# One bank for the attention sums, three common banks, and a rewritten opening order

## The chip, the cores and the metric

The kernel runs on one core of one Trainium2 chip. The metric is the device time of one execution in microseconds: the median of 16 runs is 722.01 (719.96 to 723.24). A profiled execution, recorded by the hardware, gives the times of single instructions. Engine names below are those of the profile: PE is TensorE (PEld its weight loads), DVE is VectorE, ACT is ScalarE, POOL is GpSimd, SP is SyncE. An L with a number is a line of the kernel.

## The reference

Causal attention with two kinds of heads, then a mixture of experts whose routing weights come from eight rounds of row and column normalization (Sinkhorn). Sizes: 4 batches, 8 heads, 768 positions, head width 64; 3072 tokens of width 512, 8 experts with an inner width of 1024.

```python
scores = scale * np.matmul(q, k.transpose(0, 1, 3, 2))
mask = np.where(retr, causal, causal & (is_sink | in_win))   # retrieval heads see all, others sinks and a window
a = np.exp(scores masked); a = a / a.sum(-1)
x = np.matmul(a, v)                                          # heads side by side: 3072 x 512
P = np.exp(x @ w_gate); 8 times: P /= P.sum(1); P /= P.sum(0); P *= N / E
out = sum over e of P[:, e] * (np.maximum(x @ w1[e], 0) @ w2[e])
```

## The kernel before

**Units and rounds.** Attention is cut into 24 units (b, g, u): batch b, a group g of 256 query positions, and half u of the heads (four heads, in two pairs a). A pair's scores over the keys it may see come in chunks of two key blocks: one chunk for g = 0, two for g = 1, three for g = 2. A task is one chunk of one pair, and a round is two tasks; there are 48 rounds, twelve per batch. A g = 0 unit takes one round, so two pairs end in it; in the later groups at most one pair ends in a round.

**What is done for a unit.** `emit_prep` (L249) transposes its keys and queries on PE (the tile `tr`) and copies them to `kT` on DVE (L263). `emit_scores` (L423) makes the score products (L450) into a tile `sc` of two banks, and returns two steps: the exponential on ACT (L459, PSUM to the SBUF tile `PT`), and the masking of `PT` on DVE (L468, L471). `gen_pv` (L282) makes the products of the exponentials with the values and a column of ones (L289, tile `pv`), and `normalize` inside it takes the reciprocal of the sums (L302) and multiplies (L303, into `xn`), both on DVE. `turn` (L310) transposes `xn` (L318, tile `xt`) and copies it on ACT to `xT` (L321), the experts' input.

**Fillers.** With half u = 1 of a group turned, `first_steps` (L348) queues the work of expert 0 on these 256 tokens: four first-layer steps (L357, eight products, counted as 1 each) and two second-layer steps (L371, eight products of 512 columns, counted as 2 each): 8 units per group, 96 in all. `fill(n)` takes steps from this queue, `spend(n)` (L502) tells how many units are to be left after round n. A first-layer step ends with a relu: on ACT (L362) where `late[0]` is true, else on DVE (L364). A second-layer step ends with a copy on ACT (L375). `emit_logits` (L333, tile `lgp`) makes the routing logits of a finished batch.

**PSUM.** Eight banks: `sc` two buffers of two banks, `pv` two buffers of one, and two banks under the tag "mo", which `tr`, `xt`, `lgp`, the fillers' `l1` and `l2` and the keep-warm products share in turn. `place_v` (L117), which brings the first batch's values to their place through PE, takes an `sc` buffer. Where a tile's buffers are all in use, the next writer waits for the reader of the oldest.

**Order.** The opening, from the first keep-warm products to the end of the sixth round's work, stands in a `manual_schedule` region for PE, DVE and ACT: each engine issues in the order in which the code is written. `keep_warm` (L275) adds products of 512 columns whose result nobody reads; the opening has 9 at the start and 19 later. From round 6 on (the loop `for n in range(6, rounds)`, outside the region) the framework's scheduler picks the order on each engine. POOL has its own written order of loads at the start; later loads are issued from `emit_scores`. `finish_sums` (L486) makes the value products of all pairs that are due, in the opening sometimes with the normalizing held back (`hold`). `make_far` (L236) and `make_far_all` (L222) spell out per-head factors that multiply the values of far key blocks (`emit_vfar`, L268).

**After attention** comes the Sinkhorn stretch: eight iterations on DVE, each with `fill(3)` and one small product; then the experts 1 to 7 in a seven-product scheme (L715 and L784), with PE as the engine that is never free.

Of the kernel before, what the change touches and what calls it, by code (L numbers as in the profile page):

```python
# [10 lines left out]
F32 = mybir.dt.float32  # L11
F16 = mybir.dt.float16
# [24 lines left out]
def kernel(  # L37
# [78 lines left out]

    def place_v(g):  # L117

        t = psA.tile([128, 2, 512], F32, tag="sc", bufs=2, name=f"vp_{g}")
        for n in range(2):  # L120
            rows = slice(64 * n, 64 * n + 64)
            for c in range(2):
                nc.tensor.matmul(
                    out=t[64 * c:64 * c + 64, n, :].rearrange("p (h d) -> p h d", h=H),
                    lhsT=ident16[rows, rows], rhs=vraw[g][rows, :, c, :], start=True, stop=True,
                )
        nc.scalar.activation(
            out=v_tile(0)[:, :, 2 * g:2 * g + 2, 0:D].rearrange("p h n d -> p n h d"),
            in_=t.rearrange("p n (h d) -> p n h d", h=H), func=AF.Copy, bias=0.0, scale=1.0,
        )  # L130

    def load_v_heads(b, h0, h1):
        for o in range(2):
# [85 lines left out]
                                    scalar2=None, op0=ALU.mult)  # L219
        nc.vector.tensor_copy(out=keep[:, 512:640], in_=keep[:, 256:384])  # L220

    def make_far_all():  # L222
        for n in range(2):
            nc.scalar.activation(
                out=farx[:, :, n], in_=farf[:, :, n].unsqueeze(2).broadcast_to([128, H, DV]),
                func=AF.Copy, bias=0.0, scale=1.0)
        nc.scalar.activation(out=farx[:, :, 2], in_=farx[:, :, 1], func=AF.Copy, bias=0.0, scale=1.0)

    def make_masks(js):
        for h in [2 * j + hh for j in js for hh in range(2)]:  # L230
# [5 lines left out]
    def make_far():  # L236

        for i in range(2):
            nc.scalar.activation(out=farf[:, :, i], in_=retf, func=AF.Copy, bias=0.0, scale=1.0)
        for rows in sinks:  # L240
            nc.vector.memset(farf[rows, :, 0], 1.0)

    wg16 = constp.tile([128, 4, E], F16, tag="wg16")

# [3 lines left out]

    def emit_prep(b, g, u):  # L249

        tr = psA.tile([128, 512], F32, tag="mo", bufs=2, name=f"tr_{b}_{g}_{u}").bitcast(F16)
        for i, src in enumerate(kq[b, g]):
            for a in range(2):
                for c in range(2):
                    for hh in range(2):
                        nc.tensor.transpose(
                            out=tr[64 * hh:64 * hh + 64, ts(4 * i + 2 * a + c, 128)],
                            in_=src[:, 4 * u + 2 * a + hh, c, :], identity=ident16,
                        )
        t = ap.tile([128, 2, 2, 256], F16, tag=f"kT{u}{g}", bufs=1 + (g == 0),  # L260
                    name=f"kT_{b}_{g}_{u}")
        kTs[b, g, u], qTs[b, g, u] = t[:, 0], t[:, 1]
        nc.vector.tensor_copy(  # L263
            out=t.rearrange("r i a (n c p) -> r (i a) c n p", c=2, p=64),
            in_=tr.rearrange("r (i c n p) -> r i c n p", i=4, c=2, p=64),
        )
# [7 lines left out]

    def keep_warm(lhsT, src, n):  # L275
        for _ in range(n):
            t = psA.tile([128, 512], F32, tag="mo", bufs=2, name="warm")
            nc.tensor.matmul(out=t[:, 0:src.shape[1]], lhsT=lhsT, rhs=src, start=True, stop=True)

    xns, turns = {}, []  # L280

    def gen_pv(b, g, u, a, PT, scale):  # L282

        pv = psA.tile([128, 2, 2, DV], F32, tag="pv", bufs=2, name=f"pv_{b}_{g}_{u}_{a}")
        vt, vf = vts[b], vfs.get(b)
        todo = pv_of(g)
        for i, (kj, far, sb, off) in enumerate(todo):
            for hh in range(2):
                nc.tensor.matmul(  # L289
                    out=pv[:, sb, hh, 0:D + 1], lhsT=PT[:, hh, off:off + 128],  # L290
                    rhs=(vf if far else vt)[:, 4 * u + 2 * a + hh, kj, 0:D + 1],
                    start=(i == 0 and hh == 0), stop=(i == len(todo) - 1 and hh == 1),
                    skip_group_check=True,
                )
            yield
        if a == 0:
            xns[b, g, u] = ap.tile([128, 2, 2, 2, D], F16, tag="xn", name=f"xn_{b}_{g}_{u}")
        xn = xns[b, g, u]

        def normalize():  # L300
            rc = ap.tile([128, 2, 2], F32, tag="rc", bufs=4, name=f"rc_{b}_{g}_{u}_{a}")
            nc.vector.reciprocal(out=rc, in_=pv[:, :, :, D])  # L302
            nc.vector.tensor_tensor(  # L303
                out=xn[:, a], in0=pv[:, :, :, 0:D],
                in1=rc.unsqueeze(3).broadcast_to([128, 2, 2, D]), op=ALU.mult)
            if a == 1:
                turns.append((b, g, u))
        scale.append(normalize)

    def turn():  # L310

        while turns:
            b, g, u = turns.pop(0)
            xn = xns.pop((b, g, u))
            xt = psA.tile([128, 512], F32, tag="mo", bufs=2, name=f"xt_{b}_{g}_{u}").bitcast(F16)
            for a in range(2):
                for sb in range(2):
                    nc.tensor.transpose(out=xt[:, ts(2 * a + sb, 128)], in_=xn[:, a, sb],  # L318
                                        identity=ident16)
            c0 = b * S + 256 * g  # L320
            nc.scalar.activation(  # L321
                out=xT[u][:, :, c0:c0 + 256], in_=xt[:, 0:512].rearrange("p (a c) -> p a c", a=2),
                func=AF.Copy, bias=0.0, scale=1.0)
            if u == 1:
                one, two = first_steps(b, g)
                at = 4 if (b, g) == (0, 1) else len(fillers)
                fillers[at:at] = one
                fillers.extend(two)

# [1 line left out]
    late = [False]  # L331

    def emit_logits(b):  # L333
        lgp = psA.tile([128, 512], F32, tag="mo", bufs=2, name=f"lgp_{b}")
# [12 lines left out]

    def first_steps(b, g):  # L348
# [2 lines left out]
        hT = [hp.tile([128, 512], F16, tag="hT", name=f"hT_0_{b}_{g}_{i}") for i in range(4)]  # L351

        def layer1(i):
            l1 = psA.tile([128, 512], F32, tag="mo", bufs=2, name="l1")
# [10 lines left out]
            return 1  # L365

        def layer2(sb):
            l2 = psA.tile([128, DM], F32, tag="mo", bufs=2, name="l2")
            for fc in range(8):
                o = 256 * (fc % 2) + 128 * sb  # L370
                nc.tensor.matmul(  # L371
# [111 lines left out]
            n -= done  # L483
            left[0] -= done

    def finish_sums(hold=False):  # L486
        held = []
        for (i, a), (gen, scale) in list(sums_of.items()):
            while run(gen, 1):
                pass  # L490
            del sums_of[i, a]
            held += scale
        if not hold:
            for f in held:
                f()
        return held


    rounds = len(tasks) // 2
    weights = [0] * 6 + [1] * (rounds - 6)  # L500

    def spend(n):  # L502
        fill(left[0] - (96 - 72 * sum(weights[:n + 1]) // sum(weights)))

    def sum_later(n):
        for i, a, ci in tasks[2 * n:2 * n + 2]:
# [19 lines left out]
    with tc.manual_schedule(engines=engines):  # L526
# [5 lines left out]
        round_first(4)  # L532
        r0 = scores(0)
        soften(r0, (0,))
        warm(3)
        make_masks((0, 1))
        emit_prep(*preps.pop())
        warm(2)
        place_v(0)
        r1 = scores(1)  # L540
        soften(r0, (1,))
        soften(r1, (0,))
        sum_later(0)
        warm(6)
        make_masks((2, 3))
        soften(r1, (1,))
        scale = finish_sums(True)
        emit_prep(*preps.pop())
        for f in scale:
            f()  # L550
        warm(4)
        sum_later(1)
        r2 = scores(2)
        soften(r2, (0,))
        turn()
        make_far_all()
        scale = finish_sums(True)
        soften(r2, (1,))
        for f in scale:
            f()  # L560
        sum_later(2)
        emit_prep(*preps.pop())
        emit_vfar(0, 1)
        warm(2)
        soften(scores(3))
        place_v(1)
        turn()
        finish_sums()
        sum_later(3)
        warm(2)  # L570
        soften(scores(4))
        turn()
        finish_sums()
        sum_later(4)
        soften(scores(5))
        turn()
        finish_sums()
        sum_later(5)
        emit_prep(*preps.pop())
    for n in range(6, rounds):  # L580
        soften(scores(n))
        if n == 7:
            place_v(2)
        if preps:
            emit_prep(*preps.pop())
        late[0] = n % 12 < 6
        turn()
        finish_sums()
        sum_later(n)
        if n % 12 == 2 and n > 12:  # L590
            emit_logits(n // 12 - 1)
# [308 lines left out]
```

The softmax here doesn't subtract the row's maximum and nothing guards it: scores larger than these inputs give would overflow.

## Time and profile before

| | |
|---|---|
| median of 16 runs | 722.01 us |
| the profiled execution | 719.76 us |
| its span, first to last instruction | 718.0 us |
| mean granted TensorE clock in the span | 0.993 |

Busy time in five stretches of the span, in us:

| stretch | PE | PEld | DVE | ACT | POOL |
|---|---|---|---|---|---|
| 31.0 to 58.3 (rounds of batch 0) | 25.14 | 16.57 | 18.59 | 16.96 | 7.89 |
| 58.3 to 97.4 (batch 1) | 37.02 | 24.72 | 21.77 | 29.14 | 9.09 |
| 97.4 to 136.0 (batch 2) | 36.58 | 24.80 | 21.38 | 28.81 | 4.47 |
| 136.0 to 168.0 (batch 3) | 31.18 | 20.72 | 16.89 | 24.80 | 0.00 |
| 168.0 to 192.0 (Sinkhorn) | 22.86 | 15.72 | 16.33 | 11.25 | 0.79 |

The batch borders are put roughly; the scheduler lets neighbouring rounds overlap. A row of the order of instructions reads: start, duration, engine, line, operation, what it writes and reads, shape, how many were merged; in brackets, how long the engine had been idle before it and what ended that idle time. Products are pipelined, so the busy time of PE includes their latency, and a PE that looks full may have short gaps. Idle time of an engine that isn't the one that everything waits for costs nothing.

### The profile page before, as it was taken

The numbers are of one execution on the slowest core, as the hardware profiler recorded it, in microseconds if no ns is written. First come the engines' busy times: TensorE is split into PE (matmuls) and PEld (weight loads), VectorE is DVE, ScalarE is ACT, GpSimd is POOL, SyncE is SP. The second block draws the span as 40 slices with busy tenths as digits, with TensorE's granted clock in tenths as the row PEclk, the third lists the DMA queues.
The fourth block names the chain that finished last, engine by engine and source line by source line (L and its number), as shares of the span: only waits on it lengthen the run. The fifth ranks groups of instructions, "written<-read, shape, count | busy, mean of one in ns | idle before, by whom it ended". The sixth has DMA issues, their size and how long they took to land.

```text
span 718.0 us, 17079 instructions
## 1 busy us (share of the span) xinstructions
PE 692.3 (96%) x6944; PEld 571.5 (80%) x6944; DVE 563.3 (78%) x1147; ACT 422.2 (59%) x787; POOL 151.2 (21%) x183
## 2 busy tenths in 40 slices
PE   7799999999999999999999999999999999999995
PEld 3466666666578888888888888888888888888884
DVE  6665465755779997888788878988898788877886
ACT  4767777685596555555555555555555555555550
POOL 7412040000011222212221212122221312121210
PEclk9999999999999999999999999999999999999999
DMA  9999393000443359434943495339543964245774
GB/s 179 178 175 104 31 105 31 2 1 2 76 69 63 59 85 162 78 54 72 164 87 55 74 148 96 68 60 150 101 74 56 145 107 78 48 80 111 147 158 123
DMA packets 84223, 65.61 MB, mean 91 GB/s; under 512 B 48304, under 2 KB 64688, under 8 KB 84144
## 3 DMA queue, kind: packets, MB, share of 16 engines
q0 software_dynamic: 74976, 57.17, 56.6%
q1 hardware_dynamic: 7536, 6.30, 3.7%
q8 instruction: 54, 0.88, 0.5%
q10 hardware_dynamic: 1632, 1.05, 0.5%
q14 instruction: 25, 0.20, 0.1%
HBM read 52.45 MB, written 6.29 MB: 82 GB/s over the span
## 4 chain that ended last, share of the span: by engine, by line
PE 67%; DVE 2%; issue 0%; ACT 0%; DVEq 0%
PE l1y L715 19%; PE l2y L784 19%; PE l2w L784 10%; PE l1w L715 10%; PE l2z L784 5%; PE l1z L715 5%; DVE acc L801 1%; DVE S L652 0%; DVE hT L730 0%; DVE T L661 0%; ACT hT L754 0%; ACT R L724 0%; DVEq L895 0%; ACT add L798 0%; DVEq L730 0%
## 5 line engine op out<-in xcount | busy, mean ns | idle before, releaser
L806 POOL DMA_DIRECT2D acc<-add x120 | 101.4, 845 | 381.7 <-ACT add L798 352.2
L724 ACT ACTIVATE R<-l1y 128x512 f32<-128x512 f32 x164 | 98.5, 601 | 127.6 <-PE l1y L715 92.6
L784 PEld LDWEIGHTS <-S 128*128 128x128 f16 x1344 | 131.2, 98 | 17.1 <-DVE S L652 1.2
L715 PEld LDWEIGHTS <-S 128*128 128x128 f16 x1312 | 128.3, 98 | 17.3 <-issue 2.3
L801 DVE SCALAR_TENSOR_TENSOR acc<-l2y,Pne,acc 128x256 f32<-128x256 f32 x256 | 111.2, 475 | 29.9 <-PE l2y L784 29.8
L784 PEld LDWEIGHTS <-hT 128*128 128x128 f16 x1008 | 98.6, 98 | 12.0 <-issue 0.6
L715 PEld LDWEIGHTS <-w 128*128 128x128 f16 x984 | 96.3, 98 | 12.0 <-issue 0.7
L715 PE MATMUL l1y<-T,S 128*128 128x256 f16 x656 | 98.4, 272 | 1.4 <-ACT R L724 1.4
L459 ACT ACTIVATE PT<-sc 128x1024 f16<-128x1024 f32 (+1 forms) x96 | 83.3, 925 | 14.6 <-PE sc L450 14.5
L784 PE MATMUL l2y<-T,S 128*128 128x256 f16 x672 | 87.1, 273 | 0.0
L798 ACT ACTIVATE add<-l2w,Pne 128x256 f32<-128x256 f32 x80 | 33.6, 472 | 66.0 <-PE l2w L784 64.1
L652 DVE TENSOR_TENSOR S<-hT 128x1024 f16<-128x1024 f16 x84 | 57.6, 686 | 17.1 <-ACT hT L754 14.8
L730 DVE CUSTOM_DVE_ANT_0 hT<-l1z,R 128x512 f16<-128x512 f32 x82 | 56.2, 685 | 7.5 <-ACT R L724 7.5
L730 DVE CUSTOM_DVE_ANT_0 hT<-l1w,R 128x512 f16<-128x512 f32 x82 | 56.1, 685 | 4.3 <-PE l1w L715 0.4
L730 DVE CUSTOM_DVE_ANT_0 hT<-l1y,R 128x512 f16<-128x512 f32 x82 | 55.7, 679 | 0.1
L754 ACT ACTIVATE hT<-l1y 128x512 f16<-128x512 f32 x82 | 49.0, 597 | 4.3 <-PE l1y L715 2.8
L724 ACT ACTIVATE R<-l1w 128x512 f32<-128x512 f32 x82 | 49.4, 603 | 0.1
L715 PE MATMUL l1z<-xT,w 128*128 128x256 f16 x328 | 49.4, 273 | 0.0
L715 PE MATMUL l1w<-T,S 128*128 128x256 f16 x328 | 49.4, 273 | 0.0
L715 PE MATMUL l1w<-xT,S 128*128 128x256 f16 x328 | 49.4, 272 | 0.0
L715 PE MATMUL l1y<-T,w 128*128 128x256 f16 x328 | 49.2, 272 | 0.1
L357 PE MATMUL l<-xT,w 128*128 128x256 f16 x384 | 47.7, 272 | 1.7 <-ACT xT L321 1.3
(102 smaller groups left out, 1030.3 us busy)
## 6 DMA issues: line engine op xcount, KB each, us to landing
acc<-add POOLq DMA_DIRECT2D x120, 256.0 KB, 3.3
w<-in_moe_w_dram POOLq DMA_DIRECT2D x16, 1024.0 KB, 10.4
out_dram<-acc SPq DMA_DIRECT2D x44, 128.0 KB, 2.6
k<-in_k_dram POOLq DMA_DIRECT2D x11, 256.0 KB, 5.1
q<-in_q_dram POOLq DMA_DIRECT2D x11, 256.0 KB, 5.7
v<-in_v_dram POOLq DMA_DIRECT2D x12, 192.0 KB, 7.5
acc<-in_v_dram POOLq DMA_DIRECT2D x3, 256.0 KB, 7.4
acc<-in_q_dram ACTq DMA_DIRECT2D x2, 256.0 KB, 5.2
```

The source lines that it names most:

```text
L357: nc.tensor.matmul(out=l1[:, ts(fb % 2, 256)], lhsT=w1[:, dc, ts(fb, 128)], rhs=xT[dc // 2][:, dc % 2, c0:c0 + 256], start=(dc == 0), stop ...
L459: nc.scalar.activation(out=PT[:, :, c0:c0 + width], in_=sc[:, :, 0:width], func=AF.Exp, bias=0.0, scale=SCALE,)
L652: nc.vector.tensor_tensor(out=out_, in0=a_, in1=b_, op=op)
L715: nc.tensor.matmul(out=banks[g, bank][:, f, :], lhsT=lefts1[e][k - 1][:, dc, ts(2 * g + f, 128)], rhs=rights1[c][k - 1][:, dc, :], start=( ...
L724: nc.scalar.activation(out=R[name], in_=banks[g, bank], func=AF.Copy, bias=0.0, scale=1.0)
L730: nc.vector._custom_dve(TENSOR_ADD_SAT, out=block(g, i, n), in0=banks[g, bank], in1=R[name], s0=65504.0, s1=0.0)
L754: nc.scalar.activation(out=block(g, 1, 0), in_=banks[g, "y"], func=AF.Relu, bias=0.0, scale=1.0)
L784: nc.tensor.matmul(out=banks[bank][q], lhsT=lefts2[e, c][k - 1][:, q, f, :], rhs=rights2[e][k - 1][:, f, :], start=(first and (final or q ...
L798: nc.scalar.activation(out=t[:, q, :], in_=banks[bank][q], func=AF.Copy, bias=0.0, scale=w)
L801: nc.vector.scalar_tensor_tensor(out=dst, in0=banks[bank][q], scalar=w, in1=dst, op0=ALU.mult, op1=ALU.add,)
L806: nc.gpsimd.dma_start(out=acc[c][:, i, n, :, :], in_=t, accum_op=ALU.add)
```

## The change

- The sums' tile `pv` has one buffer in place of two; the tag "mo" has three in place of two.
- `place_v` takes two "mo" tiles of one bank, one after the other, each with its own ACT copy, in place of one two-bank `sc` tile with one copy.
- `finish_sums` normalizes each pair right behind its products and can be given work to call between two pairs. In the loop that work is `fill(1)`.
- The relus go to ACT in rounds n % 12 < 2 in place of n % 12 < 6.
- `make_far_all` is gone: its three ACT copies stand at two places, two in `make_far`, the third later in the opening.
- The opening is written in another order, with 7 keep-warm products in place of 19 behind the first 9, and with four filler steps. `spend` has the quota to match (92 and 68 units in place of 96 and 72). `turn` puts the first-layer steps of group (0, 1) ahead of the two last fillers in place of behind the first four.

```diff
     def place_v(g):
 
-        t = psA.tile([128, 2, 512], F32, tag="sc", bufs=2, name=f"vp_{g}")
         for n in range(2):
+            t = psA.tile([128, 512], F32, tag="mo", bufs=3, name=f"vp_{g}_{n}")
...
-        nc.scalar.activation(
-            out=v_tile(0)[:, :, 2 * g:2 * g + 2, 0:D].rearrange("p h n d -> p n h d"),
-            in_=t.rearrange("p n (h d) -> p n h d", h=H), func=AF.Copy, bias=0.0, scale=1.0,
-        )
+            nc.scalar.activation(
+                out=v_tile(0)[:, :, 2 * g + n, 0:D], in_=t.rearrange("p (h d) -> p h d", h=H),
+                func=AF.Copy, bias=0.0, scale=1.0,
+            )
...
-    def make_far_all():
...
+    def spell_far(n, src):
+        nc.scalar.activation(out=farx[:, :, n], in_=src, func=AF.Copy, bias=0.0, scale=1.0)
...
+        for i in (1, 0):
+            spell_far(i, farf[:, :, i].unsqueeze(2).broadcast_to([128, H, DV]))
...
-        pv = psA.tile([128, 2, 2, DV], F32, tag="pv", bufs=2, name=f"pv_{b}_{g}_{u}_{a}")
+        pv = psA.tile([128, 2, 2, DV], F32, tag="pv", bufs=1, name=f"pv_{b}_{g}_{u}_{a}")
...
-                at = 4 if (b, g) == (0, 1) else len(fillers)
+                at = len(fillers) - 2 * ((b, g) == (0, 1))
...
-    def finish_sums(hold=False):
...
+    def finish_sums(between=None):
+
+        for i, ((gen, scale), key) in enumerate([(sums_of[key], key) for key in sums_of]):
+            if i and between:
+                between()
+            while run(gen, 1):
+                pass
+            del sums_of[key]
+            scale[0]()
...
-        fill(left[0] - (96 - 72 * sum(weights[:n + 1]) // sum(weights)))
+        fill(left[0] - (92 - 68 * (n - 5) // (rounds - 6)))
...
         r0 = scores(0)
         soften(r0, (0,))
-        warm(3)
         make_masks((0, 1))
         emit_prep(*preps.pop())
+        warm(3)
+        r1 = scores(1)
+        soften(r1[:1], (0,))
+        place_v(0)
+        soften(r0, (1,))
+        sum_later(0)
+        soften(r1[1:], (0,))
+        make_masks((2, 3))
+        emit_prep(*preps.pop())
         warm(2)
...
+        r2 = []
+        finish_sums(lambda: r2.extend(scores(2)))
         soften(r1, (1,))
...
+        soften(r2, (0,))
+        warm(2)
+        turn()
         sum_later(1)
...
+        emit_vfar(0, 1)
+        finish_sums(lambda: emit_prep(*preps.pop()))
+        place_v(1)
+        soften(r2, (1,))
+        sum_later(2)
+        r3 = scores(3)
+        soften(r3, (0,))
         turn()
...
+        spell_far(2, farx[:, :, 1])
         finish_sums()
+        soften(r3, (1,))
         sum_later(3)
-        warm(2)
+        fill(1)
         soften(scores(4))
-        turn()
         finish_sums()
         sum_later(4)
+        fill(1)
+        emit_prep(*preps.pop())
         soften(scores(5))
         turn()
         finish_sums()
         sum_later(5)
-        emit_prep(*preps.pop())
+        fill(2)
...
-        late[0] = n % 12 < 6
+        late[0] = n % 12 < 2
         turn()
-        finish_sums()
+        finish_sums(lambda: fill(1))
```

The opening before, where lines are left out above, ran: placing (0), round 1's scores, masks and exponentials, six keep-warms, head masks, first sums, next unit's transposes, four keep-warms, round 2's scores, turn, spelling, second sums, transposes, far values, and then one round after the other with two keep-warms between.

More of the change, by code (lines that the diff above doesn't have):

```diff
@@ L123, in place_v @@
                 nc.tensor.matmul(
-                    out=t[64 * c:64 * c + 64, n, :].rearrange("p (h d) -> p h d", h=H),
+                    out=t[64 * c:64 * c + 64, :].rearrange("p (h d) -> p h d", h=H),
                     lhsT=ident16[rows, rows], rhs=vraw[g][rows, :, c, :], start=True, stop=True,
                 )
-        nc.scalar.activation(
-            out=v_tile(0)[:, :, 2 * g:2 * g + 2, 0:D].rearrange("p h n d -> p n h d"),
-            in_=t.rearrange("p n (h d) -> p n h d", h=H), func=AF.Copy, bias=0.0, scale=1.0,
-        )
+            nc.scalar.activation(
+                out=v_tile(0)[:, :, 2 * g + n, 0:D], in_=t.rearrange("p (h d) -> p h d", h=H),
+                func=AF.Copy, bias=0.0, scale=1.0,
+            )
     def load_v_heads(b, h0, h1):
@@ L220, in make_keep @@
         nc.vector.tensor_copy(out=keep[:, 512:640], in_=keep[:, 256:384])
-    def make_far_all():
[L223 to L227, printed above, removed]
+    def spell_far(n, src):
+        nc.scalar.activation(out=farx[:, :, n], in_=src, func=AF.Copy, bias=0.0, scale=1.0)
     def make_masks(js):
@@ L249, in emit_prep @@
     def emit_prep(b, g, u):
-        tr = psA.tile([128, 512], F32, tag="mo", bufs=2, name=f"tr_{b}_{g}_{u}").bitcast(F16)
+        tr = psA.tile([128, 512], F32, tag="mo", bufs=3, name=f"tr_{b}_{g}_{u}").bitcast(F16)
         for i, src in enumerate(kq[b, g]):
@@ L276, in keep_warm @@
         for _ in range(n):
-            t = psA.tile([128, 512], F32, tag="mo", bufs=2, name="warm")
+            t = psA.tile([128, 512], F32, tag="mo", bufs=3, name="warm")
             nc.tensor.matmul(out=t[:, 0:src.shape[1]], lhsT=lhsT, rhs=src, start=True, stop=True)
@@ L314, in turn @@
             xn = xns.pop((b, g, u))
-            xt = psA.tile([128, 512], F32, tag="mo", bufs=2, name=f"xt_{b}_{g}_{u}").bitcast(F16)
+            xt = psA.tile([128, 512], F32, tag="mo", bufs=3, name=f"xt_{b}_{g}_{u}").bitcast(F16)
             for a in range(2):
@@ L333, in emit_logits @@
     def emit_logits(b):
-        lgp = psA.tile([128, 512], F32, tag="mo", bufs=2, name=f"lgp_{b}")
+        lgp = psA.tile([128, 512], F32, tag="mo", bufs=3, name=f"lgp_{b}")
         for i in range(NC):
@@ L353, in layer1 @@
         def layer1(i):
-            l1 = psA.tile([128, 512], F32, tag="mo", bufs=2, name="l1")
+            l1 = psA.tile([128, 512], F32, tag="mo", bufs=3, name="l1")
             for fb in (2 * i, 2 * i + 1):
@@ L367, in layer2 @@
         def layer2(sb):
-            l2 = psA.tile([128, DM], F32, tag="mo", bufs=2, name="l2")
+            l2 = psA.tile([128, DM], F32, tag="mo", bufs=3, name="l2")
             for fc in range(8):
@@ L484, in fill @@
             left[0] -= done
-    def finish_sums(hold=False):
-        held = []
-        for (i, a), (gen, scale) in list(sums_of.items()):
+    def finish_sums(between=None):
+        for i, ((gen, scale), key) in enumerate([(sums_of[key], key) for key in sums_of]):
+            if i and between:
+                between()
             while run(gen, 1):
                 pass
[L491 to L496, printed above, removed]
+            del sums_of[key]
+            scale[0]()
     rounds = len(tasks) // 2
-    weights = [0] * 6 + [1] * (rounds - 6)
     def spend(n):
-        fill(left[0] - (96 - 72 * sum(weights[:n + 1]) // sum(weights)))
+        fill(left[0] - (92 - 68 * (n - 5) // (rounds - 6)))
     def sum_later(n):
@@ L534 @@
         soften(r0, (0,))
-        warm(3)
         make_masks((0, 1))
         emit_prep(*preps.pop())
-        warm(2)
[L539 to L545, printed above, removed]
-        soften(r1, (1,))
-        scale = finish_sums(True)
-        emit_prep(*preps.pop())
-        for f in scale:
-            f()
-        warm(4)
-        sum_later(1)
-        r2 = scores(2)
-        soften(r2, (0,))
-        turn()
[L556 to L563, printed above, removed]
-        warm(2)
-        soften(scores(3))
-        place_v(1)
-        turn()
+        warm(3)
[7 more added lines that the diff above has]
+        emit_prep(*preps.pop())
+        warm(2)
+        r2 = []
+        finish_sums(lambda: r2.extend(scores(2)))
+        soften(r1, (1,))
+        soften(r2, (0,))
+        warm(2)
+        turn()
+        sum_later(1)
+        emit_vfar(0, 1)
[5 more added lines that the diff above has]
+        soften(r3, (0,))
+        turn()
+        spell_far(2, farx[:, :, 1])
         finish_sums()
+        soften(r3, (1,))
         sum_later(3)
-        warm(2)
+        fill(1)
         soften(scores(4))
-        turn()
         finish_sums()
         sum_later(4)
+        fill(1)
+        emit_prep(*preps.pop())
         soften(scores(5))
@@ L578 @@
         sum_later(5)
-        emit_prep(*preps.pop())
+        fill(2)
     for n in range(6, rounds):
```

## The prediction

> **What bounds the kernel now.** I read the chain of waits first, then the busy time by stretches, then the order of single instructions.
>
> ```profile
> PE 67%; DVE 2%; issue 0%; ACT 0%; DVEq 0%
> PE l1y L715 19%; PE l2y L784 19%; PE l2w L784 10%; PE l1w L715 10%; PE l2z L784 5%; PE l1z L715 5%; DVE acc L801 1%; DVE S L652 0%; DVE hT L730 0%; DVE T L661 0%; ACT hT L754 0%; ACT R L724 0%; DVEq L895 0%; ACT add L798 0%; DVEq L730 0%
> ```
>
> The end is set by TensorE in the experts (L715, L784), which the change doesn't touch. Whatever is gained or lost must shift the start of that stage, about 192 us. Before it lie the opening (to 31 us), the rounds (31 to 168) and the Sinkhorn stretch (168 to 192). TensorE is the longest engine there too: in the rounds ScalarE has 17 to 29 us of work per 27 to 39 us. So TensorE's own order counts: work removed from it, and its waits.
>
> In the Sinkhorn stretch 24 expert units fill TensorE before and after the change: nothing there.
>
> **The opening, in its written order.** Two things hold it: next unit's keys come late, and the clock.
>
> ```profile
> 12.75 0.41 PE L123 MATMUL vp<-acc,ident 64*64 64x512 f16 x4
> 14.29 0.34 PE L450 MATMUL sc<-kT 64*128 64x256 f16 x4 [0.86 <-ACT v L127]
> 14.56 1.47 PE L278 MATMUL warm<-kT,ident 128*128 128x512 f16 x6
> 17.00 0.69 DVE L263 COPY kT<-tr 128x1024 f16<-128x1024 f16 x1 [0.77 <-PE tr L256]
> 18.73 1.73 ACT L459 ACTIVATE PT<-sc 128x1024 f16<-128x1024 f32 x2 [3.09 <-PE sc L450]
> ```
>
> The value placing takes a score buffer, so half of round 1's scores wait until 14.29; six keep-warm products follow; the keys of the next unit are copied only at 17.00, and ScalarE has stood 3.09 us when round 2's exponentials start. The change gives the placing single banks, moves the next unit's transposes ahead, puts round 2's scores between the first two sums, and cuts keep-warms from 19 to 7 (the nine at the start stay).
>
> I wrote the new order out engine by engine, each step starting at the latest of its inputs, its engine and its bank, with the trace's durations (kT copy 0.69, mask of a pair 0.56 or 0.29+0.56, exp 0.76 or 0.86, normalizing 0.17+0.42, scores of a round 0.45, transposes 0.45, a first-layer step 8 x 0.109 = 0.9):
>
> ```
> step                            before         new order
> 2nd transposes (heads at 9.30)  10.92          9.53 (no warms ahead)
> its kT copied                   12.72          11.4 (masks hold VectorE to 10.66)
> round 1 scores                  13.09, 14.29   11.65 (behind 3 warms of 0.43)
> next unit's kT copied           17.69          15.1 (2 PT masks, 4 head masks ahead)
> round 2 scores                  18.29          15.15
> its exponentials                18.73-20.46    15.6-17.35
> half round 3 scores / exps      21.73 / 22.58  19.5 / 20.7 (exps behind v copies)
> xT of first two units ends      25.69          23.0
> first expert step               32.96          23.05
> round 4 scores / exps           26.26 / 26.91  23.95 / 24.1
> two more rounds' work ends      30.9           29.7, with 4 expert steps done
> ```
>
> "Rounds" here are the calls of scores; first sums start at 14.15 (values placed by 14.1), are normalized at 15.7, and the second pair enters the one bank then. At 17.3 the second unit's first sums are done and the next transposes go between; its second sums wait for VectorE (copied far values, then normalizing) until 18.9. The last two of the four expert steps start at 27.9 and 28.8, when the relus and key copy that free their banks are done. The opening gains 30.9 - 29.7 = 1.2, plus four steps of 0.9 that the rounds no longer do (their quota falls from 72 to 68 units): 3.6. Sum 4.8. The chain passes some twenty engine changes, each of which I gave 0.05 us where the trace shows 0.05 to 0.1: I take off 1.2 and say **3.6**. Below: 1.5 if the clock falls once more; above: 5.
>
> What I cost at nothing: two far spellings (L224, 0.59 each) now at 5.08 to 6.26 on ScalarE lie beside the load of the first keys, which lands at 6.35; 0.1 us more and the first transposes are late one for one. The third (0.64, 23.0 to 23.65) is hidden by round 4's scores, which end after 24. Value placing by two copies of 128x512 (row: 0.60, L375) for one of 1.02 adds 0.2 three times, the second on the path, counted. Loads: POOL's written list is the same; its first buffer wait (keys of the next batch, 12.74, behind the second transposes) ends earlier. From issue to landing in the trace: first unit's next q at 12.18 against a need at 12.65 (the one close call), the third group's q 22.10 against 25.75, w1 18.52 against 23.05, w2 28.52 against the first second-layer step after 31. SP's queue issues nothing more.
>
> [...]
>
> ```profile
> 5.60:9.00 3.40, 1.05 (x20) 0.67 (x22) 2.64 (x8) 1.99 (x4) 3.40 (x5) 0.96 1.58 225
> 9.00:12.40 3.40, 3.39 (x28) 1.46 (x25) 2.03 (x5) 1.81 (x3) 3.17 (x4) 0.54 1.82 181
> 19.20:22.60 3.40, 2.15 (x38) 1.30 (x35) 2.34 (x7) 3.37 (x7) 1.72 (x3) 1.00 1.74 188
> 22.60:26.00 3.40, 1.73 (x24) 0.93 (x23) 2.37 (x6) 3.09 (x5) 1.62 (x2) 0.97 1.25 209
> 26.00:29.40 3.40, 3.32 (x33) 1.76 (x32) 1.45 (x6) 2.48 (x3) 0.33 (x1) 0.53 1.78 182
> ```
>
> Columns: stretch, length, busy PE, PEld, DVE, ACT, POOL, granted clock. After a stretch with TensorE busy 1.05, and after one with 1.73, it runs at half clock; after 2.15 it doesn't. [...] By the rows, the new stretch 19 to 22.4 holds about 1.7 us of work (sums 0.2, placing 0.35, scores 0.45, turn 0.25, sums 0.45), as much as the one that was punished: the half-clock stretch stays, a little earlier. I go by the rows: no change. A second one would cost 1.7.
>
> **The third common bank**, in the rounds. The trace shows such a wait:
>
> ```profile
> 55.10 0.53 PE L289 MATMUL pv<-v,PT 128*128 128x65 f16 x12
> 55.30 0.56 DVE L471 TENSOR_TENSOR PT<-PT,mask 128x768 f16<-128x768 f16 x1 [0.40 <-ACT PT L459]
> 55.77 0.68 DVE L263 COPY kT<-tr 128x1024 f16<-128x1024 f16 x1
> 56.51 1.89 PE L371 MATMUL l<-w,hT 128*128 128x512 f16 x8 [0.88 <-ACT xT L321]
> 56.84 0.24 DVE L302 RECIPROCAL rc<-pv 128x4 f32<-128x4 f32 x2
> 57.05 0.75 DVE L303 TENSOR_TENSOR xn<-pv,rc 128x256 f16<-128x256 f32 x2
> ```
>
> Transposes and turn hold both banks, and the expert step stands 0.88 until one is copied out. The same gap comes at 95.56 and 136.10; 0.46 at 60.92, 99.99 and 143.63; 0.31 and 0.22 once each: 4.55 us. Some of it another wait takes over (the next scores' exponentials are late then): bounds 0 and 4.5, I take **2.3**.
>
> **One bank for the sums.** Where two sums end in one round (six times in the rounds), the second now waits until the first is normalized, and normalizing is queued on VectorE behind the round's masks and the kT copy. In the stretch above: first sums done 55.3, one step between until 56.15 (first layer) or 57.0 (second), first normalizing over at about 57.45: a stand of 1.3 or 0.45, with that round's other steps and the next transposes behind it on TensorE; but the old gap of 0.88 is gone, and these rounds are ordered by the scheduler, which may put scores there. Bounds 0 and 1.3 each, so 0 to 8; I take 0.15 each, 1.0, since the trace shows it splitting sums around other work (31.77: six sums, scores, eight sums). Single sums are close too:
>
> ```profile
> 67.80 0.17 DVE L302 RECIPROCAL rc<-pv 128x4 f32<-128x4 f32 x1
> 68.77 0.42 DVE L303 TENSOR_TENSOR xn<-pv,rc 128x256 f16<-128x256 f32 x1
> 69.37 0.28 PE L289 MATMUL pv<-vf,PT 128*128 128x65 f16 x4
> ```
>
> The bank would come free at 69.19, 0.18 us before the next sums. Taken: 0.3 in all; bounds 0 and 0.3 at each of some 30.
>
> **Relus.** Of 14 on ScalarE in the rounds (0.61) about ten move to VectorE (0.685). ScalarE, 29.1 of 39.1 us, loses 2 per batch; VectorE, 21.8, gains 2.3. Exponentials come earlier, masks and normalizing queue behind relus. Bounds 1 gained to 2 lost; taken 0.
>
> **Sum.** -3.6 - 2.3 + 1.0 + 0.3 = -4.6. The profiled execution took 719.76 (span 718.0 and 1.76 around it): 715.2. The median of the runs is 722.01, 2.25 above, so I forecast a median of **717.4**.
>
> **Rivals.**
> - *All of it comes* (0.20): opening 4.8, third bank 4.5, sums free: 722.0 - 9.3 = 712.7. For it: the scheduler has work to put in between. Against: exponentials stand behind each bank wait.
> - *The opening is hidden or eaten* (0.15): one more half-clock stretch leaves 1.9, and 1.5 more lost in the rounds than taken eats the third bank: 722.0 - 1.9 - 2.3 + 1.3 + 1.5 = 720.6. For it: stretches of 1.7 busy.
> - *The one bank becomes the bound* (0.17): 1.3 at six double sums and 0.1 at thirty single ones, 10.8 lost against 5.9 gained: 726.9; at 1.0 and 0.03, 6.9 lost, 723.0. It decides from a total of 5.9; I price it at the lower pair, 723.0. For it: VectorE is filled with relus just then. Against: idle times before normalizing of up to 2.4 us, where VectorE waited for the sums, not they for it.
>
> The forecast itself has 0.48, own range 714.5 to 719.5. Under 0.2% (1.4 us) this kernel's runs can't tell. The all-come case and the forecast are faster, of the second rival a third: 0.73; within 0.2% 0.10; slower 0.17. Range 712 to 722.8.
>
> **What would show it.** Round 2's exponentials near 15.6 and a first expert step near 23 (opening right); no wait of L371/L357 for an xT or kT copy (bank right); TensorE waiting for L303 before sums (sum bank wrong); half clock granted twice after 12 us (warms were needed). The experts' stretch should keep its length and only start earlier, near 187.4. If it starts there and the total doesn't fall, I have missed a cover in the experts.

## The result, and the profile after

The median fell from 721.79 us (44 runs, 719.89 to 724.49) to **709.61 us** (8 runs, 707.40 to 710.68): a ratio of 0.983, 95% interval 0.9817 to 0.9842. The forecast was 717.4 with a range of 712.0 to 722.8: the direction was right, but 12.2 were gained where 4.6 were forecast, and the median lies 2.4 below the range. The profiled execution of the changed kernel took 709.92 us (span 708.2), that of the kernel before 719.76.

First the chain that ended last, of the changed kernel, from its page (shares of the span by engine, then by engine and line):

```profile
PE 50%; DVE 1%; issue 0%; ACT 0%; DVEq 0%
PE l1y L706 14%; PE l2y L775 14%; PE l1w L706 7%; PE l2w L775 7%; PE l2z L775 4%; PE l1z L706 4%; DVE acc L792 1%; DVE S L643 0%; ACT R L715 0%; DVEq L886 0%
```

The same experts' products (their lines moved by nine) still set the end. The chain found covers less of the span, but the stretch hasn't changed: from the first of the experts' products to the end of the span it took 525.5 us before (192.5 to 718.0) and 525.8 after (182.4 to 708.2). All of the gain lies ahead of it, as forecast.

The opening in the order of instructions, changed kernel (start, duration, engine, line, what it writes and reads; in brackets the idle time before it and who ended it):

```profile
10.18 0.64 PE L254 MATMUL tr<-ident,k 128*64 128x128 f16 x8
12.58 0.78 PE L448 MATMUL sc<-kT 64*128 64x256 f16 x8
14.40 0.68 DVE L261 COPY kT<-tr 128x1024 f16<-128x1024 f16 x1
15.45 0.39 PE L448 MATMUL sc<-kT,kT 64*128 64x256 f16 x4
15.88 1.73 ACT L457 ACTIVATE PT<-sc 128x1024 f16<-128x1024 f32 x2 [0.28 <-PE sc L448]
19.45 0.36 PE L287 MATMUL pv<-v,PT 128*128 128x65 f16 x6 [0.71 <-DVE xn L301]
23.43 1.44 PE L355 MATMUL l<-xT,w 128*128 128x256 f16 x6 [1.59 <-ACT xT L319]
29.30 1.91 PE L355 MATMUL l<-xT,w 128*128 128x256 f16 x16
```

Beside the lines shown of before: the next unit's keys are copied at 14.40 where it was 17.00, round 2's exponentials start at 15.88 where it was 18.73, and ScalarE stood 0.28 us before them where it stood 3.09. The order forecast had the keys copied by 15.1 (here the copy ends at 15.08) and the exponentials start at 15.6. It put the expert steps behind the turn copy at 23.05; here six of the first step's eight products wait for that copy until 23.43. The opening, taken to the first scores of round 6, ends at 31.1 with four expert steps in it, where it ended at 32.2 with none.

To compare the rounds I took from both traces the distance from each TensorE product's start to the next one's, and took away the usual distance for its shape (109 ns for 256 columns, 216 for 512, 29 for a value product, and so on). Where what is left exceeds 170 ns, I call it a wait; the small rests I call switching. The rounds reach from the first scores of round 6 to the first Sinkhorn product:

```
rounds          length  products  waits (places)  switching
before          140.2   116.4     12.2 (25)       11.5
after           131.0   113.6      6.4 (15)       11.0

waits by the product that came late   before  after
expert step                           4.2     1.0
routing logits                        2.2     0.4
key/query transposes                  1.9     0.0
scores                                2.6     1.5
turn                                  1.4     1.6
sums                                  below 0.1  1.6
```

In the profiled executions: 1.0 us in the opening, 2.8 fewer products in the rounds (four steps moved into the opening, some transposes out of it), 5.8 fewer waits, 0.5 less switching, and 0.4 lost behind: 9.7 of the 9.8.

### The profile page after: what moved, and what is told of

Its sections match the earlier page's. It is cut to its first block, busy times and chain, and to the rows that moved or that the text cites. A ratio compares the mean times of both kernels' runs of the same rounds, so it can differ in the third digit from the quotient of the medians.

```text
span 708.2 us, 17061 instructions
## 1 busy us (share of the span) xinstructions
PE 687.4 (97%) x6932; PEld 569.3 (80%) x6932; DVE 568.8 (80%) x1157; ACT 417.9 (59%) x780; POOL 151.2 (21%) x183
## 3 DMA queue, kind: packets, MB, share of 16 engines
q10 hardware_dynamic: 1632, 1.05, 0.5%
## 4 chain that ended last, share of the span: by engine, by line
PE 50%; DVE 1%; issue 0%; ACT 0%; DVEq 0%
PE l1y L706 14%; PE l2y L775 14%; PE l1w L706 7%; PE l2w L775 7%; PE l2z L775 4%; PE l1z L706 4%; DVE acc L792 1%; DVE S L643 0%; ACT R L715 0%; DVEq L886 0%
## 5 line engine op out<-in xcount | busy, mean ns | idle before, releaser
L775 PEld LDWEIGHTS <-S 128*128 128x128 f16 x1344 | 131.0, 98 | 17.2 <-DVE S L643 1.2
L355 PE MATMUL l<-xT,w 128*128 128x256 f16 x384 | 49.4, 275 | 2.4 <-ACT xT L319 2.4
```

The costliest lines, as they stand in the source:

```text
L355: nc.tensor.matmul(out=l1[:, ts(fb % 2, 256)], lhsT=w1[:, dc, ts(fb, 128)], rhs=xT[dc // 2][:, dc % 2, c0:c0 + 256], start=(dc == 0), stop ...
L775: nc.tensor.matmul(out=banks[bank][q], lhsT=lefts2[e, c][k - 1][:, q, f, :], rhs=rights2[e][k - 1][:, f, :], start=(first and (final or q ...
```

## The experiments

All runs are set against runs of the kernel before on the same chip. Those medians moved from 720.15 to 722.26 between four sessions (experiments 1 to 4; 5 to 7 and the first kernel of 8; the next three of 8; the last), and each ratio moves with them. So a difference of up to some 2 us (0.003) between ratios of two sessions tells nothing; kernels of one session can be set against each other more closely.

**1. The opening alone.** From the changed kernel, banks, relus and fillers in the loop put back:

```diff
-tag="mo", bufs=3        # everywhere
+tag="mo", bufs=2
-tag="pv", bufs=1
+tag="pv", bufs=2
-        late[0] = n % 12 < 2
+        late[0] = n % 12 < 6
-        finish_sums(lambda: fill(1))   # in the loop
+        finish_sums()
```

> The new opening alone: two banks for the sums, two common banks, relus on ScalarE in rounds n % 12 < 6 and no filler between two sums, all as before. Theory A (the opening is worth what was forecast, 3.6, and the rest comes from the banks): 722 - 3.6 = 718.4, within 1. Theory B (the opening also changes what the scheduler makes of the rounds, since four steps fewer and an earlier start order them anew): 712 to 715.

715.00 us, ratio 0.9913 (0.989 to 0.9936): 6.9 below the 721.89 beside it. The number is at the upper edge of theory B (712 to 715), but only a part of B's reason is seen. By the trace the opening ends where it did (32.2) with the four steps in it, and the rounds take 135.5: 113.6 products, 10.9 waits, 11.1 switching. So in this profiled execution (715.21) it gained 4.6, of which 1.3 is fewer waits in the rounds; most of the other 2.3 is the distance between the old kernel's profiled execution (719.76) and its median here. The next section returns to that.

**2. The rounds alone.** The old opening, its first two double sums normalized at once so that one sums bank suffices; banks, relus and loop as changed.

```diff
-        scale = finish_sums(True)      # twice, its normalizing written later
+        finish_sums()
```

> The old opening (its first two double sums normalized at once, no longer held back) with the new rounds: one bank for sums, three common ones, relus on ScalarE in n % 12 < 2, a filler between two sums. Theory A: 722 less about 8 = 714, the opening missing. Theory B: 718 or more.

715.30, ratio 0.9916 (0.9895 to 0.9936): 6.6 gained; by the trace the rounds take 134.0. Together with the opening's 6.9 that is 13.5, against 12.2 for both at once: the two halves act nearly apart, and they are about equal. Theory B, that the rounds gain only through the opening, falls.

**3. The banks alone**, with old relus and no filler between, on the same old opening.

> Old opening and old rounds with the new split of the banks alone (one for sums, three common). Theory A with the third bank as the cause: 715 to 717, all but the opening. If the relus or the filler between carry it: 719 to 722. If the one bank for sums costs what the forecast took without the filler between: 721 or more.

717.59, ratio 0.9945 (0.9926 to 0.9965): 4.3 gained, though this opening ends 1.3 later than before (33.5): its sums now wait 3.1 us for the single bank, since the order there is fixed. The rounds themselves went from 140.2 to 135.9. The median is just above theory A's 717. From start to start, waits before steps, logits and transposes fell from 8.3 to 1.6, but those before scores rose from 2.6 to 5.4.

Experiments 2 and 3 ran in one session and differ only in relus and filler. Together these two are worth 2.3 us in the medians here (715.30 for 717.59; the intervals just overlap) and 1.9 in the rounds by the traces, where the waits before scores are 2.8 with them.

**4. The third common bank taken away again.** Everything as changed, one bank for the sums, two common banks; the eighth lies unused.

```diff
-tag="mo", bufs=3
+tag="mo", bufs=2
```

> The changed kernel with two common banks in place of three, one bank for the sums: the eighth bank lies unused. Theory A (third common bank): 709.6 + 6 or more, 715.5 to 719, the waits of expert steps for a key copy or turn copy back. Theory B (order, relus, fillers carry it): 709.6 to 712.

716.17, ratio 0.9925 (0.9907 to 0.9943) against 0.983 for the changed kernel: the bank is worth 6.6 us. By the traces 5.3 of that lie in the rounds, which take 136.3 for 131.0, with 11.6 us of waits, 6.6 of them before expert steps. Another 1.8 lie in the opening, which ends at 33.0 for 31.1; 0.4 come back behind the rounds. In the opening the next unit's transposes, at 13.62 in the changed kernel, now wait for the copy of the placed values:

```profile
15.08 0.64 PE L254 MATMUL tr<-ident,k 128*64 128x128 f16 x8 [0.68 <-ACT v L127]
```

The opening's share isn't clean, since here half clock was granted from 7.8 to 21.4, in the changed kernel from 23.4 to 26.8. In the rounds both had the full clock.

Who waits for whom on TensorE, first the expert steps in this kernel's rounds, then every row of the changed kernel from 31 to 159 us (us in total, times, longest):

```profile
PE l L355 <- ACT xT L319: 1.9, 2, 1.1
PE l L355 <- DVE hT L362: 1.1, 3, 0.5
PE l L369 <- ACT xT L319: 1.1, 1, 1.1
PE l L369 <- DVE hT L362: 0.5, 2, 0.3
```

```profile
PE l L355 <- ACT xT L319: 0.8, 1, 0.8
PE pv L287 <- DVE xn L301: 0.8, 3, 0.4
PE sc L448 <- ACT PT L457: 0.7, 3, 0.3
PE xt L316 <- DVE xn L301: 0.7, 2, 0.5
```

With two banks a step stands behind the reader of an earlier tile (a turn copy, or the relu of a step before) seven times or more (eight by these rows, one of which may be the data wait shown next); with three, one such row is left, and that one is no bank wait. Its place in the changed kernel:

```profile
53.42 0.40 PE L316 MATMUL xt<-ident,xn 128*128 128x128 f16 x4
53.65 0.34 PE L287 MATMUL pv<-v,PT 128*128 128x65 f16 x6
53.84 0.38 PE L355 MATMUL l<-xT,w 128*128 128x256 f16 x2
54.40 0.62 ACT L319 ACTIVATE xT<-xt 128x512 f16<-128x512 f16 x1
55.06 0.82 PE L355 MATMUL l<-xT,w 128*128 128x256 f16 x6 [0.85 <-ACT xT L319]
55.40 0.17 DVE L300 RECIPROCAL rc<-pv 128x4 f32<-128x4 f32 x1
55.60 0.42 DVE L301 TENSOR_TENSOR xn<-pv,rc 128x256 f16<-128x256 f32 x1
```

Two of the step's eight products have started at 53.84, so its bank is free. The third reads the turned values that ScalarE copies only at 54.40: a wait for data, which no bank removes. It also shows the filler between the two sums: the first six value products at 53.65, then the step, while normalizing comes at 55.40.

**5. Two banks for the sums, two common ones**, all else as changed: the price of the single sums bank.

```diff
-tag="pv", bufs=1
+tag="pv", bufs=2
```

(beside the edit of experiment 4)

> The changed kernel with two banks for the sums and two common banks, as before; opening, relus and fillers between as changed. Against the run with one bank for sums and two common ones (716.2) it prices the single sums bank alone. Forecast's price (1.3 lost by one bank): 714.9. If one bank costs nothing: 716.2, within 0.7. If it costs what the upper bound said: 712 or less. Against the opening alone (715.0) it prices relus and fillers between: same within 0.7 if they are worth nothing.

717.07, ratio 0.9938 (0.9922 to 0.9954), against 0.9925 (0.9907 to 0.9943) with one: beside two common banks the single bank costs nothing that can be told. But there the sums hardly wait in either kernel (about 0.2 us in the rounds); the 1.6 us of waits before sums come only with the third common bank, and a second sums bank beside three common ones was not run (with the four of the scores that makes nine, where both kernels use eight). So what those 1.6 us cost in the changed kernel stays open.

With two common banks, relus on VectorE and fillers between didn't help: experiment 1, without them, was at 715.00 (0.9913). The 2.1 us between the two are more than the 0.7 expected, but lie between two sessions.

**6. Relus on ScalarE again, with three common banks.**

```diff
-        late[0] = n % 12 < 2
+        late[0] = n % 12 < 6
```

> The changed kernel with the relus on ScalarE in rounds n % 12 < 6 again. Forecast (worth nothing, minus 1 to plus 2): 709 to 711. If VectorE's relus are what lets the exponentials keep up with three common banks: 712 to 715.

709.58, ratio 0.9832 (0.981 to 0.9854): the same. The rounds took 131.1 for 131.0.

**7. No filler between two sums in the loop.**

```diff
-        finish_sums(lambda: fill(1))
+        finish_sums()
```

> The changed kernel with nothing written between two sums in the loop. If the scheduler orders the products anyway (the forecast's reason for a low price of the one bank): 709.6 within 0.7. If the filler between is what hides the wait for normalizing: six places at 0.45 to 1.3, 712 to 717.

710.42, ratio 0.9848 (0.983 to 0.9866). Its interval overlaps the changed kernel's, and its rounds took 131.6, with 7.0 us of waits for 6.4: the filler is worth some 0.6 by the trace, not told by the runs. The prices of 2.4 and more are out. The new relus and the filler are thus worth little when either is taken away alone; the changed kernel without both was not run, and in the old order both together were worth 2.3.

**8. The early expert steps and the keep-warms.** Four kernels: the changed one without the four early steps (quota and place of the steps as before); without the seven later keep-warms; with 19 of them; with neither steps nor keep-warms. And the kernel before without its 19.

```diff
-        fill(1)        # and fill(1), fill(2): a_noearly, a_bare
-        warm(3)        # and warm(2), warm(2): a_nowarm, a_bare
+        warm(6)        # in place of warm(3); and 9 more in three places: a_warm19
-        warm(3)        # and all others after the first nine: b_nowarm
```

> The changed kernel without the four expert steps in the opening; the loop has the quota of before (96 and 72 units) and the old place for the group's first-layer steps. Forecast: these steps fill time that stands idle otherwise, 3.6 of products: 709.6 + 3 = 712.6 or a little more. If the gain of the opening lies in its order alone: 710 to 711. If early steps also keep the scheduler's rounds fed: 714 or more.

709.83, ratio 0.9836 (0.9819 to 0.9854): the early steps are worth nothing that can be told. Without them the opening ends at 27.2, and the rounds take 134.5 for 131.0. The 3.5 us that the steps save there they cost in the opening, to within 1 us: it ends with them at 31.1 in the changed kernel, and at 29.9 and 30.1 in experiments 6 and 7, whose opening is the same code. These differ in the clock. In the changed kernel half clock fell on the steps, and six products took 1.44; in experiment 6 it didn't:

```profile
23.35 0.81 PE L355 MATMUL l<-xT,w 128*128 128x256 f16 x6 [1.59 <-ACT xT L319]
```

What the steps displace is seen in the fifth and sixth calls of scores of this kernel:

```profile
22.03 0.40 PE L448 MATMUL sc<-kT,kT 64*128 64x256 f16 x4 [0.62 <-ACT PT L457]
23.55 3.38 ACT L457 ACTIVATE PT<-sc 128x1024 f16<-128x1024 f32 x4
24.67 0.39 PE L448 MATMUL sc<-kT,kT 64*128 64x256 f16 x4 [0.41 <-ACT PT L457]
```

Scores come at 22.03 and 24.67 where they came at 24.80 and 28.15 with the steps ahead of them (24.10 and 26.56 in experiment 6), and ScalarE goes through four exponentials without a gap (3.38 us). The step at 23.43 in the changed kernel, which waited for the turn copy, held the scores queued behind it on TensorE.

> The changed kernel without the seven later keep-warm products. By the forecast's rows (stretches with about 1.7 us of work or less are followed by half clock): one or two half-clock stretches more between 9 and 27, each worth up to 1.7 if TensorE is the bound there: 711 to 713. If the new opening hangs on VectorE and ScalarE: the same, 708.5 to 710.3, whatever clock is granted.

709.48, ratio 0.9857 (0.9838 to 0.9877), beside runs of before at 720.15. In absolute time that is the changed kernel's, and in the range expected if the opening hangs on VectorE and ScalarE; by the ratio it would be 2 us slower, but the changed kernel did not run beside those runs of before.

> The changed kernel with 12 more keep-warm products in the opening, 19 as before. If the dropped ones were worth time only as work on TensorE (12 x 0.22): up to 2.6 slower, 710 to 712.2. If they keep the clock and that is worth more: 708 or less. If TensorE isn't the bound in the opening: the same.

710.33, ratio 0.9859 (0.9844 to 0.9874). Set against the kernel with none, in the same session, 19 later keep-warms cost 0.9 in the medians, and the intervals overlap: too little to be told, and within both the first expectation and the last. The opening ends at 31.6 by the trace, without them at 30.1. In both the rounds take 131.0, as in the changed kernel.

> The kernel before without its 19 later keep-warm products, nothing else. If part of the change's gain beyond the forecast is that the old opening lost more to the clock and to the products themselves: 717 to 720. If they kept the clock: 723 to 726. If neither: 721 to 722.3.

718.03, ratio 0.9967 (0.9956 to 0.9979), nine runs against fourteen of one session: 2.1 gained by nothing but leaving them out. The old opening then ends at 30.4 for 32.2.

> The changed kernel with neither the seven later keep-warm products nor the four early expert steps (quota of before): only the new order is left of the opening. Each alone was worth nothing. If the opening is bound by the chain through VectorE and ScalarE, both together are too: 709 to 710.3. If the early steps took the keep-warms' place as work for the clock: 711 or more. If both only stood in the way: 708 or less, and this is the best version.

709.59, ratio 0.9834 (0.9818 to 0.985). The order alone gives all of the opening's gain. No version can be told to be faster than the changed kernel.

## Why the prediction was wrong

**What held.** The experts' and Sinkhorn's stretches only moved. The table of the new opening was right within 0.7 us down to the third round's scores, but for round 1's scores (11.65 forecast, 12.58 measured). Its sum was right in the profiled execution: 3.6 forecast, 1.0 earlier and 2.8 us of products out of the rounds measured. One cover put at nothing failed there: the two far spellings ran from 5.74 to 6.92, the copy of the first keys behind them on ScalarE began at 6.82 (6.37 before), and the first transposes at 7.48 (7.05 before). Relus alone were worth nothing, as taken. The price of the single sums bank, 1.3, was of the right size as waits (1.6 us before sums in the rounds); what they cost net was not shown.

**The term that failed: the third common bank, "Bounds 0 and 4.5, I take 2.3".** In the rounds, for which the term stood, the bank was worth 5.3 in the changed kernel (experiment 4) and 4.3 in the old order (experiment 3): about twice what was taken, at the upper bound or above. Two mistakes. The bound was added up from the bracketed idle times, and those count from the end that the rows show for the product before. At the place shown in the prediction twelve value products start at 55.10, 29 ns apart, so the last at 55.43; the step starts at 56.51. The order lost 1.05 there, and the bracket shows 0.88. A product of 65 columns ends 0.19 after its start in this trace, while the next starts after 0.03. At 60.92 it is 0.67 for a bracket of 0.46:

```profile
60.08 0.39 PE L450 MATMUL sc<-kT,kT 64*128 64x256 f16 x3
60.92 0.74 PE L338 MATMUL lgp<-wg,xT 128*128 128x8 f16 x24 [0.46 <-DVE kT L263]
```

The eight places that the forecast added to 4.55 come to 6.1 from start to start. Another 2.2 have no bracket or weren't counted. In all, the waits before steps, logits and transposes are 4.2 + 2.2 + 1.9 = 8.3 before and 1.4 after: 6.9 gone.

The second mistake is the halving, "Some of it another wait takes over". In the changed kernel waits before scores went down with the others, from 2.6 to 1.5, and only 1.6 came up before sums. With the banks alone (experiment 3) the forecast's reason is seen: waits before scores grew by 2.8. With the new relus and the filler added (experiment 2) they were back at 2.8. So whether another wait takes over hung on the order of the rest, and the forecast had priced that rest at nothing.

**The second error: the distance from the profiled execution to the median.** The forecast carried 2.25 over unchanged. The profiled execution of before (719.76) lies under all of the first 16 runs (719.96 at the least), and the changed kernel's (709.92) lies 0.3 above its median. So 2.6 of the missing 7.8 are no cost of any step; the other 5.2 are nearly all waits in the rounds, 5.8 fewer where the forecast had a net of 1.0.

The granted clock of the single runs shows where much of the distance comes from. In the experiments' sessions the kernel before ran 37 times. The 12 runs with a mean granted clock of 0.990 or less took 722.06 to 724.50, the 25 with more took 719.51 to 721.89. The profiled execution, at 0.993, is of the second kind. In all fourteen profiled executions half clock (0.50) was recorded only in the opening (from 8.71 to 12.12 and 25.77 to 29.19 before, from 23.42 to 26.83 in the changed kernel) and in the last 5 us. Without the later keep-warms the time no longer follows the clock: five runs at 0.981 to 0.987 took 716.87 to 719.14, four at 0.996 to 0.998 took 717.14 to 719.30. In the trace of before, three keep-warms from 9.53 on started 0.40 and 0.43 apart (granted clock 0.50), six from 14.56 on 0.21 to 0.23 apart (1.00). From these an estimate: 19 of them on TensorE's path lose up to 4 us more where half clock falls on all. This fits, but no trace of a run at a low clock was kept to show it product by product.

**Right sum, wrong reason: the early steps.** The forecast said that four steps fill time that is idle. Experiment 8 shows that they take about their full time, and that the order alone ends the opening 5.0 earlier (in an execution with a mean granted clock of 0.999; the one of before, with 0.993, had two half-clock stretches of 3.4 us there). The table put them in where TensorE was free, but wrote the scores of the next round behind them, and those are what ScalarE waits for. That the sum still came out is luck.

**The rivals.** The first, that all of it comes, was nearest (712.7), still 3.1 above the result. Its reason, that the scheduler has work to put in between, holds for the changed kernel; with the banks alone (experiment 3) other waits took over a part. The one sums bank as the bound fell (1.6 us of waits), and so did the hidden opening (6.9 gained by it alone).

## What to carry to other kernels

Price a wait of TensorE from the start of one product to the start of the next, less the usual distance, not from the idle time that a row shows; at the places compared here the row leaves out 0.17 to 0.21 us each, a sixth to a third of the wait. Where several short-lived tiles rotate through two PSUM banks and TensorE waits for their readers, a third bank can be worth more than a second one for a tile that is used once per round: here 5.3 and 4.3 us in the rounds for the third, and nothing that can be told for the second beside two common ones (717.07 with it, 716.17 without). And look where the profiled execution lies among the runs, in time and in granted clock, before adding its distance to the median to another kernel.

## What the runs showed of the hardware

A half-clock stretch (granted clock 0.50 for 3.4 us) came at 23.42 in the changed kernel, about where the rows of the prediction had put it. In the 3.4 us before it TensorE was busy 1.78 us and never stood for more than 1.59 us at once. Of the two half-clock stretches of before, the 3.4 us ahead of 8.71 have TensorE busy 0.83 us, with 1.78 us as the longest stand, those ahead of 25.77 have 1.50 us busy, with 1.35 us. But the busy time just before doesn't decide it alone. Stretches of 3.4 us in the changed kernel, then in experiment 6, whose opening is the same code, then in the kernel without later keep-warms (columns as in the prediction: length, busy PE, PEld, DVE, ACT, POOL, granted clock):

```profile
20.00:23.42 3.42, 1.78 (x32) 1.22 (x29) 2.49 (x8) 3.24 (x6) 1.61 (x2) 1.00 1.62 192
23.42:26.83 3.41, 3.40 (x31) 2.19 (x31) 1.75 (x4) 1.86 (x3) 1.11 (x2) 0.50 1.25 207
```

```profile
21.08:24.50 3.42, 1.77 (x24) 1.18 (x22) 2.06 (x7) 2.74 (x5) 1.89 (x3) 1.00 1.43 202
24.50:27.91 3.41, 3.29 (x65) 2.48 (x62) 2.54 (x7) 2.64 (x3) 0.82 (x1) 1.00 1.51 194
```

```profile
16.30:19.72 3.42, 1.90 (x42) 1.30 (x39) 3.10 (x8) 1.88 (x3) 0.69 (x1) 1.00 1.51 193
19.72:23.13 3.41, 3.14 (x32) 1.94 (x33) 1.99 (x8) 2.84 (x5) 1.62 (x3) 0.50 1.66 188
```

Stretches with TensorE busy 1.78 and 1.90 us were followed by half clock (0.50), one with 1.77 was not (1.00). Ahead of 13.18 us the clock figures of the changed kernel's rows don't fit its products: they say 1.00 from 9.76 to 13.18, but its keep-warms from 11.18 on started 0.40 and 0.43 apart, as those of before did at 0.50. So that the forecast's stretch came where it said was in part luck, and what decides stays open.

What such a stretch costs depends on what it falls on. From the waiting expert step to round 6's scores the changed kernel took 7.7 us with half clock from 23.42, experiments 6 and 7 took 6.5 each with the full clock there. Without later keep-warms and with half clock from 19.72 to 23.13 the opening ended at 30.1, as in experiment 7, where two such stretches lay between 7.7 and 14.5.

Nor did leaving out keep-warms gain by a better clock. The nine runs of before without its later ones had a mean granted clock of 0.990, fourteen with them in the same session 0.993, and those without were 2.1 us faster. In the new opening it was 0.994 with none and 0.997 with 19 (four runs each), with no gain in time.
